# Moments of later columns taken ahead of most of the first fold, roots in three batches of four, folds and first transforms moved

## The chip, the cores and the metric

The kernel runs on one core of a Trainium2 chip. The metric is device microseconds (us) of one execution. A time is the median of several runs; most runs of one kernel agree within 0.3%. "Span" is the profiled execution from its first to its last instruction; it is about 1.7 to 1.8 us shorter than the timed value.

Names: PE is TensorE, DVE is VectorE, ACT is ScalarE, POOL is GpSimd, SP is SyncE.

## The reference

```python
x  = A_x                                  # 1 x 2048 x 512, bf16
xn = layernorm(x)                         # over the 512 features
a  = irfft2(rfft2(xn) * (w_r + 1j*w_i))   # over rows and features
b  = (gelu(xn @ w_gate) * (xn @ w_up)) @ w_down    # inner width 1792
return x + a + b
```

## The kernel before

The 2048 rows are 16 "columns" of 128 rows. Four columns make a block. PE computes the gated unit (`glu`: gate and up products, 14 slices of the inner width for each block) for block 0, then blocks 1 to 3, and then the down projection. The spectral part (fold, products `bp` with the row transform, feature transforms, filter, inverse) is interleaved with the units of `glu`. Before a block's units can start, its four columns are normalized: moments on DVE, `1/sqrt` by Newton steps on POOL ("roots"), normalization on ACT, transposes by DMA.

```python
def rsqrt(V, y, var, n):                  # V is POOL for columns 4 to 15
    v = pc.tile([P, n], F32, name=f"v{n}"); t = ...
    V.tensor_scalar(out=v[:], in0=var, scalar1=EPS, ...)
    V.tensor_scalar(out=yi, in0=vi, scalar1=-0.5, scalar2=float(0x5F3759DF), ...)
    for _ in range(3):                    # Newton steps, 4 operations each on POOL
        ...
def moments(c):                           # DVE: "stats", then "mv"
    tc.keep_in_program_order(V.bn_stats(out=stats[:], in_=x_t[:, c, :]))
    V.bn_aggr(out=mv[:, c, :], in_=stats[:])
# ... (cut)
def normalize(c):                         # columns 4 to 15: ACT, waits for rstd and nb of POOL
    tc.keep_in_program_order(
        nc.scalar.activation(out=xn[:, c, :], in_=x_t[:, c, :], func=AF.Identity,
                             bias=nb[:, c:c + 1], scale=rstd[:, c:c + 1]))
def fold(cg):                             # DVE, four steps: A, A, xf, xf; needs xn of 4 columns
    ...
def pstep(cg, q):                         # PE: products bp of fold cg; ACT copies them to Bs
    ...
def glu(c0, n, fc):                       # PE: 4 + 4 matmuls
    gp = ps.tile(..., name="g_ps", tag="G", bufs=2)
    up = ps.tile(..., name="u_ps", tag="U", bufs=2)
    # ... matmuls (cut)
    nc.scalar.activation(out=ge[:], in_=gp[:], func=AF.Gelu_apprx_tanh)              # ACT frees g_ps
    nc.vector.tensor_tensor(out=hT[sb, fc][:, o:o + w], in0=up[:], in1=ge[:], ...)   # DVE frees u_ps

# the schedule: (time in units, task); a unit of four columns and one slice counts 1.724
for c0, n, t in ((4, 4, 8), (8, 8, 14)):
    for c in range(c0, c0 + n):
        j = c - c0
        tasks.append((t + 0.8 * j, lambda c=c: moments(c)))
        tasks.append((t + n + 5 + 0.9 * j, lambda c=c: (normalize(c), transposes(c, 1))))
    tasks.append((t + n - 0.5, lambda c0=c0, n=n: scales(nc.gpsimd, c0, n)))
for cg in range(4):
    t = (8, 21, 30.5, 34)[cg]
    tasks.append((t, lambda cg=cg: fold(cg)))
    for q in range(4):
        tasks.append((t + (3 + q if cg < 2 else 1.5 + 0.6 * q), lambda cg=cg, q=q: pstep(cg, q)))
t0, dt = 38, 5.5                          # first feature transforms
```

Each engine works through its instructions in one fixed order, made when the program is built; an instruction that waits holds up everything behind it on that engine. And `g_ps` and `u_ps` have two buffers each: PE can be one unit ahead of ACT's gelu and of DVE's `hT`, not more.

Of the kernel before, what the change touches and what calls it, by code (L numbers as in the profile page):

```python
# [10 lines left out]
P = 128  # L11
BF16 = mybir.dt.bfloat16
F32 = mybir.dt.float32
# [110 lines left out]
def kernel(  # L124
# [11 lines left out]
    nc = tc.nc  # L136
# [11 lines left out]
    pc = ctx.enter_context(tc.tile_pool(name="pc", bufs=1))  # L148
    ps = ctx.enter_context(tc.tile_pool(name="ps", bufs=2, space=bass.MemoryType.PSUM))
    pw = ctx.enter_context(tc.tile_pool(name="pw", bufs=2))  # L150
# [79 lines left out]

    def rsqrt(V, y, var, n):

        v = pc.tile([P, n], F32, name=f"v{n}")
        t = pc.tile([P, n], F32, name=f"t{n}")
        V.tensor_scalar(out=v[:], in0=var, scalar1=EPS, scalar2=None, op0=ALU.add)
        vi, yi = v[:].bitcast(I32), y.bitcast(I32)
        V.tensor_scalar(out=yi, in0=vi, scalar1=-0.5, scalar2=float(0x5F3759DF), op0=ALU.mult, op1=ALU.add)
        for _ in range(3):
            V.tensor_tensor(out=t[:], in0=y, in1=y, op=ALU.mult)
            if V is nc.vector:  # L240
                V.scalar_tensor_tensor(out=t[:], in0=v[:], scalar=-0.5, in1=t[:],
                                       op0=ALU.mult, op1=ALU.mult)
                V.scalar_tensor_tensor(out=y, in0=t[:], scalar=1.5, in1=y,
                                       op0=ALU.add, op1=ALU.mult)
                continue
            V.tensor_tensor(out=t[:], in0=v[:], in1=t[:], op=ALU.mult)
            V.tensor_scalar(out=t[:], in0=t[:], scalar1=-0.5, scalar2=1.5, op0=ALU.mult, op1=ALU.add)
            V.tensor_tensor(out=y, in0=t[:], in1=y, op=ALU.mult)
# [5 lines left out]
    def moments(c):  # L254
        V = nc.vector
        stats = pw.tile([P, V.BN_STATS_DIM], F32, name="stats")
        tc.keep_in_program_order(V.bn_stats(out=stats[:], in_=x_t[:, c, :]))  # L257
        V.bn_aggr(out=mv[:, c, :], in_=stats[:])

    def scales(V, c0, n):  # L260
        r, b = rstd[:, c0:c0 + n], nb[:, c0:c0 + n]
        rsqrt(V, r, mv[:, c0:c0 + n, 1], n)
        if c0 >= 4:
            V.tensor_tensor(out=b, in0=mv[:, c0:c0 + n, 0], in1=r, op=ALU.mult)
            V.tensor_scalar(out=b, in0=b, scalar1=-1.0, scalar2=None, op0=ALU.mult)  # L265

    def normalize(c):
        if c < 4:
            nc.vector.tensor_scalar(out=xn[:, c, :], in0=x_t[:, c, :], scalar1=mv[:, c, 0:1],
                                    scalar2=rstd[:, c:c + 1], op0=ALU.subtract, op1=ALU.mult)  # L270
        else:
# [3 lines that stand above are left out]
# [26 lines left out]
    def transposes(c0, n):  # L301
        if c0 < 4:
            tp = ps.tile([P, NE, n, P], BF16, name="tp", tag="S", bufs=4)
            for j in range(n):
                for e in range(NE):
                    nc.tensor.transpose(tp[:, e, j, :], xn[:, c0 + j, e * P:(e + 1) * P], ident)  # L306
            return nc.vector.tensor_copy(out=xnT[0][:, :, c0:c0 + n, :], in_=tp[:])
        else:
            for j in range(c0, c0 + n):
                nc.sync.dma_start_transpose(out=xnT[j // 4][:, :, j % 4, :], in_=xn[:, j, :])  # L310
# [4 lines left out]
    def fold(cg):  # L315
        V = nc.vector
        xs = xn[:, 4 * cg:4 * cg + 4, :]
        lo, hi = xs[:, :, 0:256], xs[:, :, 511:255:-1]
        A = pw.tile([P, 4, 2, 256], BF16, name="A", bufs=1)
        V.tensor_tensor(out=A[:, :, 0, :], in0=lo, in1=hi, op=ALU.add)  # L320
        V.tensor_tensor(out=A[:, :, 1, :], in0=lo, in1=hi, op=ALU.subtract)
        xf = pw.tile([P, 4, 4, P], BF16, name="xf")
        V.tensor_tensor(out=xf[:, :, 0:4:3, :], in0=A[:, :, :, 0:128], in1=A[:, :, :, 255:127:-1],  # L323
                        op=ALU.add)
        V.tensor_tensor(out=xf[:, :, 2:0:-1, :], in0=A[:, :, :, 0:128], in1=A[:, :, :, 255:127:-1],
                        op=ALU.subtract)
        fold_out[cg] = xf

    def pstep(cg, q):
        xf = fold_out[cg]  # L330
        bp = ps.tile([P, 4, P], F32, name="bp", tag="S", bufs=4)
        for j in range(4):
            nc.tensor.matmul(bp[:, j], lhsT=xf[:, j, q, :], rhs=RF_t[:, 4 * cg + j, :],  # L333
                             start=True, stop=True)
        o = Bs[:, q].rearrange("p g c r a -> p (c r) g a")[:, 8 * cg:8 * cg + 8]
        evac(o, bp[:].rearrange("p c (r g a) -> p (c r) g a", r=2, a=4))
# [174 lines left out]


    tasks = [(20, load_tables), (28, gather_tables)]
    for c0, n, t in ((4, 4, 8), (8, 8, 14)):
        for c in range(c0, c0 + n):
            j = c - c0
            tasks.append((t + 0.8 * j, lambda c=c: moments(c)))
            tasks.append((t + n + 5 + 0.9 * j, lambda c=c: (normalize(c), transposes(c, 1))))
        tasks.append((t + n - 0.5, lambda c0=c0, n=n: scales(nc.gpsimd, c0, n)))
    for cg in range(4):  # L520
        t = (8, 21, 30.5, 34)[cg]
        tasks.append((t, lambda cg=cg: fold(cg)))
        for q in range(4):
            tasks.append((t + (3 + q if cg < 2 else 1.5 + 0.6 * q), lambda cg=cg, q=q: pstep(cg, q)))
    tasks.append((36, tables_fix))
    t0, dt = 38, 5.5
    for i, g in enumerate((1, 2, 3, 4, 5, 6, 7, 0)):
        tasks.append((t0 + dt * i, lambda g=g: dstep(2 * g)))
        tasks.append((t0 + dt * i + 1, lambda g=g: dstep(2 * g + 1)))
# [50 lines left out]
```

## Time and profile before

185.42 us median (185.33 to 185.53, 4 runs).

| read from | what | value |
|---|---|---|
| page, part 1 | PE busy | 172.2 of 183.8 us (94%) |
| page, part 1 | DVE / ACT / POOL busy | 116.1 / 97.8 / 17.2 us |
| timeline of PE | first matmul | 5.68 us |
| timeline of PE | third set of transposes to first inverse product | 15.03 to 124.25: 109.2 us |

The last row is the stretch in which the change acts. Its two ends in the timeline of PE:

```profile
15.03 0.72 PE L306 MATMUL tp<-CT,xn 128*128 128x128 bf16 x8
...
124.25 0.83 PE L445 MATMUL yp<-CT,Gs 128*128 128x128 bf16 x12
```

Both kernels do the same matmuls in it, so its length is a good measure of what PE lost there. "Lost" below is time between the starts of two matmuls beyond the usual step (0.216 us for 512 columns, 0.055 for 128).

The view of windows of the kernel before, two stretches; the columns are the stretch, its length, then busy time and number of instructions of PE, PE's weight loads, DVE, ACT and POOL, then granted clock, DMA share and GB/s:

```profile
14.50:36.20 21.70, 21.57 (x160) 14.31 (x158) 19.25 (x50) 12.75 (x26) 3.28 (x17) 1.00 0.68 203
36.20:60.14 23.94, 22.78 (x143) 11.22 (x144) 14.27 (x23) 18.90 (x34) 13.69 (x32) 1.00 0.66 121
```

PE is full up to 36 us and loses over 1 us after it. The timeline of PE (start us, length us, engine, line, operation, output<-inputs, sizes, count; in brackets the idle time and what ended it) names the two large losses: at 36.0 us block 1 waits for transposed columns, and at 48.2 us the products of the third fold wait for `xf` of DVE.

```profile
35.15 1.03 PE L480 MATMUL u_ps<-xnT,Wu_sb 128*128 128x512 bf16 x4
36.72 1.02 PE L477 MATMUL g_ps<-xnT,Wg_sb 128*128 128x512 bf16 x4 [0.55 <-DMA xnT<-xn]
...
47.98 0.38 PE L477 MATMUL g_ps<-xnT,Wg_sb 128*128 128x512 bf16 x1
48.96 0.40 PE L333 MATMUL bp<-RF_t,xf 128*128 128x128 bf16 x4 [0.60 <-DVE xf L323]
```

The timeline of POOL shows the first and last operation of each of the two root batches, and two operations in the middle of the second:

```profile
24.46 0.24 POOL L235 TENSOR_SCALAR v<-mv 128x4 f32<-128x4 f32 x1 [24.03 <-DVE mv L258]
...
28.70 0.23 POOL L265 TENSOR_SCALAR nb<-nb 128x4 f32<-128x4 f32 x1
36.16 0.60 POOL L235 TENSOR_SCALAR v<-mv 128x8 f32<-128x8 f32 x1 [7.22 <-DVE mv L258]
...
37.40 0.20 POOL L239 TENSOR_TENSOR t<-rstd 128x8 f32<-128x8 f32 x1
...
37.97 0.55 POOL L247 TENSOR_SCALAR t<-t 128x8 f32<-128x8 f32 x1
...
41.73 0.24 POOL L265 TENSOR_SCALAR nb<-nb 128x8 f32<-128x8 f32 x1
```

The first batch takes 24.46 to 28.93 us, the second 36.16 to 41.97 us. The operations of one batch have the same work, but some take 0.20 us and others 0.48 to 0.60.

### The profile page before, as it was taken

Reading aid. Unit: us, or ns where it says so; the run is one execution under the profiler, and the core shown is the slowest. Engines: PE = TensorE matmul, PEld = TensorE weight load, DVE = VectorE, ACT = ScalarE, POOL = GpSimd, SP = SyncE. Lnnn points to the kernel's source line nnn. Section 1 sums busy time; section 2 is a strip of 40 time slices with the busy share of each in tenths; the row PEclk is TensorE's granted clock in tenths of the full one; section 3 lists DMA queues with packets and bytes.
Section 4 is the critical chain, followed back from the end, with each engine's and each line's share of the span. In section 5 each row is a group of like instructions: output and inputs, shape, how many; then the busy total and the mean of one; then the engine's idle time right before and its main releaser. Section 6 shows DMA issues by size and latency. Waiting matters only on the chain.

```text
span 183.8 us, 3059 instructions
## 1 busy us (share of the span) xinstructions
PE 172.2 (94%) x1080; PEld 92.7 (50%) x1080; DVE 116.1 (63%) x273; ACT 97.8 (53%) x181; POOL 17.2 (9%) x52
## 2 busy tenths in 40 slices
PE   0699999899899999999999999999999999999991
PEld 0598974354445544554555554445445445445440
DVE  2679959972954599679778879835541541541611
ACT  2533568559888986988988875453211211211100
POOL 0000042177642000000000000000000000000000
PEclk9999999999999999999999999999999999999998
DMA  4999971404995001201392210100122221221210
GB/s 147 325 384 382 339 181 30 86 0 110 227 136 159 0 13 44 62 14 43 80 356 83 59 48 13 44 13 2 61 83 67 78 86 62 76 95 60 83 57 29
DMA packets 22062, 19.37 MB, mean 105 GB/s; under 512 B 8288, under 2 KB 20576, under 8 KB 22048
## 3 DMA queue, kind: packets, MB, share of 16 engines
q1 hardware_dynamic: 20816, 17.22, 33.2%
q0 software_dynamic: 416, 1.32, 3.1%
q10 hardware_dynamic: 816, 0.66, 1.1%
q8 instruction: 8, 0.13, 0.3%
q14 instruction: 6, 0.05, 0.1%
HBM read 13.41 MB, written 2.10 MB: 84 GB/s over the span
## 4 chain that ended last, share of the span: by engine, by line
PE 83%; DVE 4%; DMA 3%; POOL 3%; issue 3%; ACT 2%; ACTq 0%
PE y_ps L490 26%; PE g_ps L477 22%; PE u_ps L480 22%; DMA Wu_sb<-in_B_w_up_dram 3%; PE dp L346 2%; PE ep L358 2%; PE yp L445 2%; PE gp L430 2%; PE y_ps L492 2%; DVE hT L484 2%; PE bp L333 2%; ACT xn L273 1%; ACT ge L483 1%; DVE stats L257 1%; PE tp L306 1%
## 5 line engine op out<-in xcount | busy, mean ns | idle before, releaser
L477 PE MATMUL g_ps<-xnT,Wg_sb 128*128 128x512 bf16 (+2 forms) x276 | 62.3, 347 | 1.1 <-DMA xnT<-xn 0.5
L480 PE MATMUL u_ps<-xnT,Wu_sb 128*128 128x512 bf16 (+2 forms) x276 | 60.9, 344 | 0.1
L490 PE MATMUL y_ps<-Wd_sb,hT 128*128 128x512 bf16 x224 | 51.0, 379 | 0.0
L484 DVE TENSOR_TENSOR hT<-u_ps,ge 128x512 bf16<-128x512 f32 (+2 forms) x69 | 40.1, 583 | 15.0 <-PE u_ps L480 7.5
L483 ACT ACTIVATE ge<-g_ps 128x512 bf16<-128x512 f32 (+2 forms) x69 | 35.5, 520 | 21.2 <-PE g_ps L477 19.6
L480 PEld LDWEIGHTS <-Wu_sb 128*128 128x128 bf16 x276 | 26.6, 101 | 23.1 <-DMA Wu_sb<-in_B_w_up_dram 0.4
L477 PEld LDWEIGHTS <-Wg_sb 128*128 128x128 bf16 x276 | 25.8, 102 | 19.6 <-issue 2.0
L490 PEld LDWEIGHTS <-hT 128*128 128x128 bf16 x224 | 21.3, 98 | 23.1
L495 DVE TENSOR_TENSOR y_sb<-y_ps,y_sb 128x512 bf16<-128x512 f32 x16 | 11.1, 692 | 30.2 <-PE y_ps L492 30.2
L451 ACT CAST yf<-yp 128x512 bf16<-128x512 f32 x16 | 9.2, 587 | 37.3 <-PE yp L445 37.3
L361 ACT CAST E<-ep 64x512 bf16<-64x512 f32 x32 | 18.5, 579 | 3.7 <-PE ep L358 3.4
L339 ACT CAST Bs<-bp 128x512 bf16<-128x512 f32 x16 | 9.0, 586 | 3.4 <-PE bp L333 3.4
L339 ACT CAST ds<-dp 128x512 bf16<-128x512 f32 x16 | 9.2, 607 | 1.2 <-PE dp L346 1.2
L273 ACT ACTIVATE xn<-x_t,nb,rstd 128x512 bf16<-128x512 bf16 x12 | 9.4, 810 | 0.4 <-POOL nb L265 0.4
L339 ACT CAST Gs<-gp 128x512 bf16<-128x512 f32 x16 | 8.6, 591 | 1.4 <-PE gp L430 1.4
L257 DVE BATCH_NORM_STATS2 stats<-x_t 128x6 f32<-128x512 bf16 x14 | 9.2, 667 | 0.0
L383 DVE TENSOR_TENSOR X<-E 128x512 bf16<-128x512 bf16 x8 | 3.4, 426 | 8.6 <-ACT E L361 8.6
L306 PE MATMUL tp<-CT,xn 128*128 128x128 bf16 x16 | 2.0, 266 | 5.8 <-DVE xn L291 5.7
L445 PEld LDWEIGHTS <-Gs 128*128 128x128 bf16 x64 | 4.8, 98 | 3.3
L492 PE MATMUL y_ps<-yt,RI_t 128*128 128x512 bf16 x16 | 6.1, 379 | 0.0
L346 PE MATMUL dp<-CT,Bs 128*128 128x128 bf16 x64 | 6.0, 219 | 0.0
L333 PE MATMUL bp<-RF_t,xf 128*128 128x128 bf16 x64 | 5.4, 219 | 0.6 <-DVE xf L323 0.6
(67 smaller groups left out, 120.3 us busy)
## 6 DMA issues: line engine op xcount, KB each, us to landing
y_sb<-in_A_x_dram SPq DMA_DIRECT2D x16, 128.0 KB, 2.1
F<-F SPq DMA_DIRECT2D x32, 64.0 KB, 2.0
out_dram<-y_sb SPq DMA_DIRECT2D x16, 128.0 KB, 1.7
Wd_sb<-in_B_w_down_dram SPq DMA_DIRECT2D x1, 1792.0 KB, 8.8
x_t<-in_A_x_dram SPq DMA_DIRECT2D x3, 512.0 KB, 11.7
Wg_sb<-in_B_w_gate_dram SPq DMA_DIRECT2D x1, 768.0 KB, 9.0
Wu_sb<-in_B_w_up_dram SPq DMA_DIRECT2D x1, 768.0 KB, 10.6
Wg_sb<-in_B_w_gate_dram SPq DMA_DIRECT2D x2, 256.0 KB, 5.1
```

The source lines that it names most:

```text
L257: tc.keep_in_program_order(V.bn_stats(out=stats[:], in_=x_t[:, c, :]))
L273: nc.scalar.activation(out=xn[:, c, :], in_=x_t[:, c, :], func=AF.Identity, bias=nb[:, c:c + 1], scale=rstd[:, c:c + 1]))
L339: nc.scalar.copy(out=o, in_=i)
L346: nc.tensor.matmul(dp[:, q // 2, q % 2, :], lhsT=Bs[:, q, G].rearrange("p c r a -> p (c r a)"), rhs=FQ[q], start=(q == 0), stop=(q == 3), ...
L361: nc.scalar.copy(out=E[64 * h:64 * h + 64, r], in_=ep[64 * r:64 * r + 64])
L477: nc.tensor.matmul(gp[:], lhsT=Wg_sb[:, e, fc * P:(fc + 1) * P], rhs=rhs[:, e, :], start=(e == 0), stop=(e == NE - 1))
L480: nc.tensor.matmul(up[:], lhsT=Wu_sb[:, e, fc * P:(fc + 1) * P], rhs=rhs[:, e, :], start=(e == 0), stop=(e == NE - 1))
L483: nc.scalar.activation(out=ge[:], in_=gp[:], func=AF.Gelu_apprx_tanh)
L484: nc.vector.tensor_tensor(out=hT[sb, fc][:, o:o + w], in0=up[:], in1=ge[:], op=ALU.mult)
L490: nc.tensor.matmul(y_ps[:], lhsT=hT[sb, f][:, cl * P:(cl + 1) * P], rhs=Wd_sb[:, f, :], start=(f == 0), stop=False)
L492: nc.tensor.matmul(y_ps[:], lhsT=late["RI"][:, c, :], rhs=late["yt"][:, c, :], start=False, stop=True)
L495: nc.vector.tensor_tensor(out=y_sb[:], in0=y_ps[:], in1=y_sb[:], op=ALU.add)
```

## The change

Intent: take the moments of columns 4 to 7 earlier, so that block 1 doesn't wait; split the second root batch so that columns 8 to 11 don't wait for 12 to 15; place folds and transforms accordingly.

```diff
-        v = pc.tile([P, n], F32, name=f"v{n}")
-        t = pc.tile([P, n], F32, name=f"t{n}")
+        v = pw.tile([P, n], F32, name=f"v{n}")
+        t = pw.tile([P, n], F32, name=f"t{n}")
@@ the schedule
-    for c0, n, t in ((4, 4, 8), (8, 8, 14)):
-        for c in range(c0, c0 + n):
+    for c0, tm, ts, tx in ((4, 6, 9.5, 14.3), (8, 15, 18.5, 23.5), (12, 19, 23, 28)):
+        for c in range(c0, c0 + 4):
             j = c - c0
-            tasks.append((t + 0.8 * j, lambda c=c: moments(c)))
-            tasks.append((t + n + 5 + 0.9 * j, lambda c=c: (normalize(c), transposes(c, 1))))
-        tasks.append((t + n - 0.5, lambda c0=c0, n=n: scales(nc.gpsimd, c0, n)))
+            tasks.append((tm + 0.8 * j, lambda c=c: moments(c)))
+            tasks.append((tx + 0.9 * j, lambda c=c: (normalize(c), transposes(c, 1))))
+        tasks.append((ts, lambda c0=c0: scales(nc.gpsimd, c0, 4)))
     for cg in range(4):
-        t = (8, 21, 30.5, 34)[cg]
+        t = (12, 22, 29.5, 34)[cg]
@@
-    t0, dt = 38, 5.5
+    t0, dt = 39.5, 5.5
```

The tiles `v4` and `t4` are now used by three batches; `pw` holds two buffers of each name, `pc` only one. The first two folds come later in the schedule, the third one unit sooner, the transforms 1.5 units later.

## The prediction

> **What bounds it.** TensorE. The table of five stretches shows it busy 8.2 of the first 14.5 us, 21.57 of 21.70 (to 36.2), 22.78 of 23.94 (to 60.1), then gapless to 124.4. The change can only win back PE time lost between 15 and 60 us. By start-to-start times in PE's timeline (a 512-column matmul takes 0.216 us, a set of four 0.86, a fold product `bp` of four 0.22) the losses are: 0.71 us at 36.0 (block 1 waits for the transposed `xnT`, landing 36.59), 0.77 + 0.2 at 48.2 (third fold's `bp` waits for `xf`), and about 0.8 in small slips from 53 to 59.6, where products and single matmuls alternate. Sum about 2.5 us, 1.3% of 185.4.
>
> **What it moves.** Nothing is removed; POOL gets 16 more small operations (three root batches of 4 instead of 4 and 8). The static order shows: moments of columns 4 to 7 go ahead of three of the first fold's four DVE steps, and need not wait for data (landed at 12.75 us). The first fold's products move behind a 512-column unit; the third fold's `bp` stand after the 4th unit of block 1 on PE instead of the 7th; the alternation is gone.
>
> **Walk with traced durations** (moment pair 0.68 to 0.81 us, fold step 0.60, `hT` 0.34 or 0.59, normalize 0.71, gelu 0.49, copy 0.48, roots 4.5 a batch; an estimate). Moments 4 to 7 are done at 21.6 instead of 24.4, roots at 26.2 to 27.2, transposes land by about 35, before PE asks at 36.1: the 0.71 us gap goes. Roots may take up to 1 us longer because fold steps on DVE now run beside them: in the old second batch POOL operations took 0.48 to 0.60 us beside fold steps and 0.20 otherwise, which agrees with the Trainium skill, "SBUF — State Buffer", section "SBUF: two separate sides", on the exclusive port pair of VectorE and GpSimd. But moments, first and second folds now share 28 to 39 us with `hT` on one in-order DVE, so the `hT` at the block boundary comes near 39 us: PE waits 0.4 to 1 us. The second root batch ends at 38.8 to 40.3 (before, all eight at 41.97), the third at 43 to 45, later than before. ACT does xn 8 to 11 with gelus and copies between, so the third fold's `xf` comes at 46 to 47.7 (before 48.9), while PE reaches its `bp` already at 44 to 45.8: a wait of 1 to 2 us, larger than 0.77. Net over 15 to 60 us: 0.1 us gained to 1.4 lost. The constants look tuned, which argues for a gain; I weigh the two.
>
> **Prediction: 185.8 us**, 8 in 10 between 184.2 and 187.2. Faster by over 2%: 0.02; within 2%: 0.94; slower by over 2%: 0.04.
>
> **What would show it.** Right: no PE wait for `xnT` at 36 us; moments of columns 4 to 7 from 17.5 us; POOL batches from near 21.6, 34 to 35 and 39 to 40; a PE wait for `hT` near 38 to 40; a PE wait of over 1 us for the third fold's `xf` between 44 and 48; PE gapless from 60 us. Wrong: PE busy from 36 to 60 would mean about 183 us.
>
> **What would make it wrong.** If the second roots end before 38.5, the main wait falls below 1 us. If the transforms, shifted 1.5 schedule units later, delay the inverse at 124.4, it costs about 0.5 us.

## More of the kernel before

ACT hardly waits for the second batch here; its timeline:

```profile
42.00 0.81 ACT L273 ACTIVATE xn<-x_t,nb,rstd 128x512 bf16<-128x512 bf16 x1 [0.37 <-POOL nb L265]
```

## The result

186.79 us median (186.73 to 187.27, 4 runs) against 185.42. The ratio is 1.0066, with a 95% interval of 1.0043 to 1.009: within 2%, and a little slower beyond noise. (A ratio is the mean time of one kernel's runs over the mean of the other's of the same rounds, so it is not quite the ratio of the medians.) Executions over 1.5% slower than the fastest of the same kernel are left out of the means.

The same two stretches of the changed kernel, in the view of windows:

```profile
14.50:36.20 21.70, 21.10 (x157) 14.27 (x157) 18.29 (x44) 12.21 (x26) 5.18 (x19) 1.00 0.70 206
36.20:60.14 23.94, 21.05 (x132) 10.78 (x133) 14.86 (x28) 17.87 (x32) 15.14 (x46) 1.00 0.53 122
```

DVE and ACT do no more work than before; PE loses more. (The trace of this run lacks 18 of PE's 1080 matmuls, one about every 9 us, so a PE busy sum is slightly low; the length of the stretch doesn't suffer from that.) The stretch from the third transposes to the first inverse product is longer by 1.62 us, 110.83 against 109.21, which is the result; what lies outside it differs by 0.4 us the other way. (In the profiled runs, the part from the first inverse product to the end takes 59.5 to 59.6 us in three, the kernel before, e1 and e10, and 59.1 to 59.2 in the other eleven. So this 0.4 us doesn't go with the change; why it comes and goes was not looked into. Where a time and a stretch differ by 0.4 us below, it is this.) Its two ends in the timeline of PE, the changed kernel:

```profile
15.00 0.72 PE L306 MATMUL tp<-CT,xn 128*128 128x128 bf16 x8
...
125.83 0.83 PE L445 MATMUL yp<-CT,Gs 128*128 128x128 bf16 x12
```

The timeline of PE at the places that answer to those of before:

```profile
33.85 1.02 PE L480 MATMUL u_ps<-xnT,Wu_sb 128*128 128x512 bf16 x4 [0.43 <-DVE hT L484]
...
36.44 1.03 PE L477 MATMUL g_ps<-xnT,Wg_sb 128*128 128x512 bf16 x4
...
40.14 1.02 PE L480 MATMUL u_ps<-xnT,Wu_sb 128*128 128x512 bf16 x4 [0.47 <-DVE hT L484]
...
44.11 1.02 PE L477 MATMUL g_ps<-xnT,Wg_sb 128*128 128x512 bf16 x3 [0.26 <-ACT ge L483]
44.97 1.03 PE L480 MATMUL u_ps<-xnT,Wu_sb 128*128 128x512 bf16 x4
47.83 0.40 PE L333 MATMUL bp<-RF_t,xf 128*128 128x128 bf16 x4 [1.83 <-DVE xf L323]
```

The wait of block 1 for the transposed columns is gone: its first set starts at 36.44, right behind the set before it. But PE now waits for `hT` (33.85 and 40.14), for a gelu (44.11), and 1.83 us for `xf` of the third fold (47.83), where the kernel before waited 0.60.

The timeline of POOL, first and last operation of each of the three batches, and one operation beside a fold step:

```profile
21.63 0.58 POOL L235 TENSOR_SCALAR v<-mv 128x4 f32<-128x4 f32 x1 [21.19 <-DVE mv L258]
...
26.93 0.23 POOL L265 TENSOR_SCALAR nb<-nb 128x4 f32<-128x4 f32 x1
35.16 0.23 POOL L235 TENSOR_SCALAR v<-mv 128x4 f32<-128x4 f32 x1 [7.99 <-DVE mv L258]
...
35.75 0.55 POOL L239 TENSOR_TENSOR t<-rstd 128x4 f32<-128x4 f32 x1
...
40.12 0.23 POOL L265 TENSOR_SCALAR nb<-nb 128x4 f32<-128x4 f32 x1
40.43 0.23 POOL L235 TENSOR_SCALAR v<-mv 128x4 f32<-128x4 f32 x1
...
44.68 0.23 POOL L265 TENSOR_SCALAR nb<-nb 128x4 f32<-128x4 f32 x1
```

The first batch starts 2.8 us earlier than before, at 21.63. The second ends at 40.35, only 1.6 us earlier than the old one, although it has half the columns; the third ends at 44.91, 2.9 us later than all of them ended before. The timeline of ACT shows what the second batch does to it:

```profile
35.77 0.60 ACT L483 ACTIVATE ge<-g_ps 128x512 bf16<-128x512 f32 x1 [1.51 <-PE g_ps L477]
40.39 0.81 ACT L273 ACTIVATE xn<-x_t,nb,rstd 128x512 bf16<-128x512 bf16 x1 [4.02 <-POOL nb L265]
41.11 0.57 ACT L483 ACTIVATE ge<-g_ps 128x512 bf16<-128x512 f32 x1
...
47.97 0.62 ACT L483 ACTIVATE ge<-g_ps 128x512 bf16<-128x512 f32 x1
```

ACT stands 4.02 us before xn of column 8, from 36.37 to 40.39. Behind it in the queue is the gelu of block 1's first unit (41.11), whose product was complete at 37.5 us (its set starts at 36.44 in the timeline of PE). From 40.4 to about 53 us ACT then has no gap: it works off what piled up.

The waits for `hT` begin earlier, and in a similar way. ACT waits 0.73 us for the first roots, the gelu behind this runs from 29.10 us, and DVE waits 1.41 us for that gelu; the timelines of ACT and of DVE:

```profile
27.20 0.81 ACT L273 ACTIVATE xn<-x_t,nb,rstd 128x512 bf16<-128x512 bf16 x1 [0.73 <-POOL nb L265]
```

```profile
29.71 0.69 DVE L484 TENSOR_TENSOR hT<-u_ps,ge 128x512 bf16<-128x512 f32 x1 [1.41 <-ACT ge L483]
```

From 29.71 to 40.09 us DVE has no gap. PE loses 0.38 (one missing record taken off), 0.25 and 0.64 us, 1.27 in all, at 33.85, 37.55 and 40.14, each time before a set for `u_ps`, which waits until an `hT` frees a buffer. The gelus that these `hT` need had run by 36.4 us, so these 1.27 us don't come from the 4.02 us wait of ACT.

### The profile page after: what moved, and what is told of

It is laid out like the page before. It is cut to its first block, busy times and chain, and to the rows that moved or that the text cites. A ratio compares the mean times of both kernels' runs of the same rounds, so it can differ in the third digit from the quotient of the medians.

```text
span 185.0 us, 3057 instructions
## 1 busy us (share of the span) xinstructions
PE 170.8 (92%) x1062; PEld 93.0 (50%) x1080; DVE 116.3 (63%) x273; ACT 97.7 (53%) x181; POOL 20.5 (11%) x68
## 4 chain that ended last, share of the span: by engine, by line
PE 85%; DVE 4%; issue 3%; POOL 2%; ACT 2%; DMA 2%; ACTq 0%
PE y_ps L490 26%; PE g_ps L477 23%; PE u_ps L480 23%; PE yp L445 2%; PE dp L346 2%; PE gp L430 2%; PE ep L358 2%; PE y_ps L492 2%; DMA x_t<-in_A_x_dram 2%; PE bp L333 2%; PE tp L306 1%; DVE hT L484 1%; ACT ge L483 1%; DVE stats L284 1%; ACT Bs L339 1%
## 5 line engine op out<-in xcount | busy, mean ns | idle before, releaser
L477 PE MATMUL g_ps<-xnT,Wg_sb 128*128 128x512 bf16 (+2 forms) x264 | 60.1, 345 | 1.4 <-DVE xnT L307 0.5
L333 PEld LDWEIGHTS <-xf 128*128 128x128 bf16 x64 | 4.4, 98 | 4.7 <-DVE xf L323 2.3
L445 PE MATMUL yp<-CT,Gs 128*128 128x128 bf16 x64 | 5.9, 219 | 0.1
```

What stands on the lines that cost most here:

```text
L333: nc.tensor.matmul(bp[:, j], lhsT=xf[:, j, q, :], rhs=RF_t[:, 4 * cg + j, :], start=True, stop=True)
L445: nc.tensor.matmul(yp[:, q], lhsT=Gs[:, q, c], rhs=IQ[q], start=(q == 0), stop=(q == 3), skip_group_check=True)
L477: nc.tensor.matmul(gp[:], lhsT=Wg_sb[:, e, fc * P:(fc + 1) * P], rhs=rhs[:, e, :], start=(e == 0), stop=(e == NE - 1))
```

## The experiments

Theory after the result: PE's losses between 33 and 50 us come from the chain moments, roots, normalize, fold, and from instructions standing in order behind a wait in it. Rivals: the fold and transform times; the place of the third fold's products on PE; a plain lack of DVE or ACT throughput; waiting roots because of the port pair that the prediction names.

Before each run the built instruction orders were compared, because moving one task can let the scheduler reorder others. Where "the order is the same" is said, that was checked on the built program.

All runs, with the PE stretch of the profiled run (third transposes to first inverse product). The ratio is to the kernel before on the same chip.

| run | time us | ratio (95%) | chip | PE stretch us |
|---|---|---|---|---|
| kernel before | 185.42 | | first | 109.21 |
| changed kernel | 186.79 | 1.0066 (1.0043 to 1.009) | first | 110.83 |
| a0_again | 186.65 | 1.0057 (1.0036 to 1.0078) | A | 110.80 |
| e1_two_steps | 184.78 | 0.9962 (0.994 to 0.9984) | A | 108.51 |
| e2_third_fold_later | 186.58 | 1.0056 (1.0032 to 1.008) | A | 110.49 |
| e3_before_two_steps | 184.65 | 0.996 (0.9935 to 0.9986) | A | 108.76 |
| e4_fold_times_back | 188.00 | 1.001 (0.9971 to 1.0049) | B | 112.13 |
| e5_normalize_later | 185.97 | 0.9904 (0.9864 to 0.9945) | B | 110.23 |
| e6_moments_into_gap | 185.02 | 0.9852 (0.9813 to 0.9892) | B | 109.08 |
| e7_moments_all_early | 186.11 | 0.9908 (0.987 to 0.9946) | B | 110.28 |
| a1_again | 186.74 | 1.0057 (1.0044 to 1.0071) | C | 110.80 |
| e8_gap_again | 185.21 | 0.9983 (0.9967 to 0.9999) | C | 108.95 |
| e9_third_sooner | 183.26 | 0.9877 (0.9862 to 0.9892) | C | 107.22 |
| e10_third_sooner_two_steps | 183.08 | 0.9872 (0.9855 to 0.9889) | C | 106.86 |

On chip A the kernel before ran at 185.38 us, on C at 185.67, but on B at 187.66 (187.09 to 189.07). Why is open: its four slowest runs there had a granted clock of 0.986 to 0.989, but the other seven, at 0.995 to 1.0, still took 187.09 to 187.84. The other kernels did not show it, as far as one repeat can tell: e6 on B and its repeat e8 on C have 185.02 and 185.21. So the ratios of chip B are not used; its four runs are compared with each other and by their PE stretch.

### a0_again and a1_again: the changed kernel once more

No edit. Expected:

> The changed kernel itself, for reference on the same chip. It should repeat: about 1.2 to 1.4 us over the kernel before, PE waiting 1.83 us for the third fold's xf near 46 to 48 us, ACT waiting 4.0 us for the second root batch. If the loss of 0.7% is noise of one chip, it will be under 0.3% here.

> The changed kernel once more, so that the two versions below are compared with it and with the kernel before on one chip (on the last chip the kernel before ran at 187.7 us, 2 us above the other chips, while the others did not look slow). Expected 186.6 to 186.9 if the chip is like the first two, with the 4.0 us wait of ACT for the second roots.

Measured: 1.0057 both times, and the same PE stretch of 110.80 us. The loss is real and not one of a chip. (a1_again's profiled run, the slowest of its six with 188.0 us, started its third transposes 1.1 us later than the others; the stretch after that is unchanged.)

### e1_two_steps: shorten only the roots

```diff
-        for _ in range(3):
+        for _ in range(3 if V is nc.vector else 2):
```

> The changed kernel with two Newton steps instead of three on POOL: each root batch has 4 operations less, about 1.1 us (0.28 us each). The order on PE, DVE and ACT is the same as in the changed kernel. Theory (the loss is the wait of PE's static third-fold products for a chain moments, roots, normalize, fold): the wait of 1.83 us falls to about 0.5, most of the 0.43 and 0.47 us waits for hT go too, and the time falls 1.3 to 1.8 us, to about 185.2. Rival (the loss is VectorE being full between 28 and 39 us, or the later transforms): the time stays within 0.4 us of the changed kernel, since DVE's work is the same.

The result stays correct. Measured: 184.78 against 186.65, so 1.87 us faster, with the order on PE, DVE and ACT the same; a little more than expected. The second roots end at 37.82 instead of 40.35 us, and ACT's wait for them shrinks from 4.02 to 2.07 us; its 0.73 us wait for the first roots is gone, and of the 1.27 us that PE lost to `hT`, 0.43 are left. The stretch is 2.29 us shorter. The timelines of ACT and of PE in this run:

```profile
37.85 0.81 ACT L273 ACTIVATE xn<-x_t,nb,rstd 128x512 bf16<-128x512 bf16 x1 [2.07 <-POOL nb L265]
```

```profile
45.29 0.40 PE L333 MATMUL bp<-RF_t,xf 128*128 128x128 bf16 x4 [1.05 <-DVE xf L323]
```

The wait for `xf` is still 1.05 us, not the 0.5 expected. What follows: root latency is on the critical path (it sets when PE can go on). DVE's work and the instruction order did not change, so a lack of DVE throughput alone can't be the cause.

### e2_third_fold_later: move only the place where the wait shows

```diff
-        t = (12, 22, 29.5, 34)[cg]
+        t = (12, 22, 31.5, 34)[cg]
```

> The changed kernel with the third fold scheduled 2 units later (31.5 instead of 29.5): on PE its products stand after the 6th unit of block 1 instead of the 4th; DVE and ACT orders barely differ. Theory (PE's static place of these products makes the wait): the 1.83 us wait for xf disappears; ACT's backlog of gelus gives part of it back as waits for ge near 48 us, so about 1.0 us is won, about 185.8. Rival (the stage is limited by ACT or DVE throughput, the place does not matter): no gain, within 0.3 us of the changed kernel.

Measured: 186.58 against 186.65, no gain. My theory lost this point. The wait for `xf` did vanish, as expected, but the timeline of PE shows most of it back in other places (the first line is a wait that the changed kernel has too, at 44.11):

```profile
44.24 1.02 PE L477 MATMUL g_ps<-xnT,Wg_sb 128*128 128x512 bf16 x3 [0.26 <-ACT ge L483]
...
46.40 1.02 PE L477 MATMUL g_ps<-xnT,Wg_sb 128*128 128x512 bf16 x4 [0.28 <-ACT ge L483]
...
48.78 1.02 PE L477 MATMUL g_ps<-xnT,Wg_sb 128*128 128x512 bf16 x4 [0.40 <-ACT ge L483]
...
50.50 0.83 PE L333 MATMUL bp<-RF_t,xf 128*128 128x128 bf16 x12
...
53.91 0.40 PE L333 MATMUL bp<-RF_t,xf 128*128 128x128 bf16 x4 [0.20 <-ACT Bs L339]
```

New are the waits for gelus at 46.40 and 48.78 (0.28 and 0.40) and for a copy of ACT at 53.91 (0.20), with smaller slips between those. ACT is without a gap from 40.5 to 53.0 us in this run too, behind the same 4.02 us wait. So the third fold's products are only where the delay of ACT's queue shows; the cause is upstream. That made the theory sharper: ACT stands in order behind a root result, and the work behind it piles up.

### e3_before_two_steps: are roots critical in the kernel before too?

Same edit as e1, on the kernel before.

> The kernel before with two Newton steps instead of three on POOL, instruction order on the other engines the same. Theory (the chain through the roots also made the waits of the kernel before, 0.71 us for the transposes and 0.77 for xf): both shrink by up to their whole size, the time falls 0.8 to 1.5 us to about 184.2. Rival (only the new arrangement is sensitive to the roots): no change over 0.3 us.

Measured: 184.65 against 185.38, 0.73 us faster, just under the expected range. The stretch is 0.45 us shorter; the rest of the difference lies outside it. The wait for `xf` shrank (0.77 and 0.2 us lost before, 0.34 and 0.15 now), but the wait for the transposed columns did not. The first roots end at 27.64 us there and xn of column 4 starts at 28.75: on ACT it stands behind a gelu that waits for PE. Here an earlier result was of no use to an instruction that wasn't next in its queue.

Set beside e1 this says more: with the shorter roots in both, the changed kernel takes 184.78 us and the kernel before 184.65 on the same chip, with stretches of 108.51 and 108.76. So nearly all of the 1.27 us that the change cost on this chip (186.65 against 185.38) hangs on how long the roots take.

### e4_fold_times_back: undo the moved folds and transforms

```diff
-        t = (12, 22, 29.5, 34)[cg]
+        t = (8, 21, 30.5, 34)[cg]
@@
-    t0, dt = 39.5, 5.5
+    t0, dt = 38, 5.5
```

> The changed kernel with the fold and transform times of the kernel before: only the new moments, roots and normalize times are left. New theory (ACT's in-order queue puts the gelu of block 1's first unit behind xn of column 8, which waits 4.0 us for the second roots; the backlog after it is the loss): that order stays, so the loss stays, 186.2 to 186.9 us. Rival (the moved folds and transforms cost the time): back to about 185.4.

Measured: 188.00, on the chip where the others were not slow; its stretch is 112.13 us, 1.3 longer than the changed kernel's. So the moved folds and transforms were not what cost the time; with the new moments they saved some. How much is less certain: the run was not repeated on another chip, and on this one the kernel before, which has the same fold times, ran slow for a reason that is open. The expected 186.2 to 186.9 was too low. ACT waits 4.40 us for the second roots in this run, and PE's waits for a gelu are longer (0.70 and 1.41 us):

```profile
42.05 1.02 PE L477 MATMUL g_ps<-xnT,Wg_sb 128*128 128x512 bf16 x4 [0.70 <-ACT ge L483]
...
47.07 1.02 PE L477 MATMUL g_ps<-xnT,Wg_sb 128*128 128x512 bf16 x3 [1.41 <-ACT ge L483]
```

The opposite half, the kernel before with the new fold times, could not be run whole: with the third fold at 29.5 it would read column 11 before that is normalized (at 27 + 3 × 0.9 = 29.7), and the simulator refuses the program for reading a part of `xn` that was not yet written.

### e5_normalize_later: take the gelu out from behind the wait

```diff
-    ... (8, 15, 18.5, 23.5), ...
+    ... (8, 15, 18.5, 25.5), ...
```

> The changed kernel with the normalizations of columns 8 to 11 issued 2 units later (25.5 instead of 23.5): ACT now does one gelu and one copy of block 1 in the idle time before xn of column 8; DVE's order is nearly the same; on PE the third fold's products stand as in the run e2_third_fold_later. New theory: the gelu no longer waits for the roots, about 1 us less backlog, so 0.7 to 1.2 us better than e2_third_fold_later, about 185.6. Rival (the root results are simply too late, whatever stands before them in ACT's queue): within 0.3 us of that run's 186.6.

Measured: 185.97, against e2's 186.58 on another chip; by the stretch, 110.23 against 110.49, the gain is only 0.26 us. ACT's longest wait for roots fell to 0.96 us, as expected. But PE then waits 1.16 us for a gelu at 47.93; this gelu starts on ACT at 47.30, behind two normalizations in a row, and two more follow it. This fits the theory of the queue, with normalizations now piled up a few us later, but it is not a proof; the verdict is unclear. Removing a wait from ACT's queue without having the roots earlier gains little.

### e6_moments_into_gap and its repeat e8_gap_again: have the second roots early

DVE had idle time of 1.3 and 1.4 us between 25 and 29.7 us in the changed kernel. The edit puts the moments of columns 8 to 11 there:

```diff
-    ... (8, 15, 18.5, 23.5), ...
+    ... (8, 11.5, 14.5, 19.5), ...
```

> The changed kernel with the moments of columns 8 to 11 moved 3.5 units earlier, into the 2.7 us in which DVE idles between 25 and 29.7 us, and their roots and normalizations 4 units earlier; columns 12 to 15, folds and transforms as in the changed kernel, and PE's order identical to it. Theory (roots of columns 8 to 11 are late because their moments stand behind hT on DVE): roots end near 34 instead of 40.3, no ACT wait of 4 us, no PE wait for xf or ge over 0.3 us; 183.2 to 184.0, better than both kernels. Rival (DVE or ACT has too much work between 28 and 52 us in any order): no better than 186.

> e6_moments_into_gap again: 184.7 to 185.2 us; against the changed kernel on the same chip 1.5 to 2 us faster, against the kernel before about 0.3% faster or the same. Its ACT waits 3.0 us for the third roots, PE 1.1 and 0.4 us for gelus near 48 and 50 us.

Measured: 185.02 and 185.21. Against the changed kernel on the same chip C, e8 is 1.5 us faster. PE's order is the same as in the changed kernel, so this gain is of DVE's and ACT's orders and of the earlier roots. The second roots end at 33.64 (e6), ACT doesn't wait for them, and the waits for `xf` are gone. The expected 183.2 to 184.0 was missed, because the third roots were now in the way; the timeline of ACT in e6:

```profile
41.61 0.60 ACT L483 ACTIVATE ge<-g_ps 128x512 bf16<-128x512 f32 x1
45.18 0.81 ACT L273 ACTIVATE xn<-x_t,nb,rstd 128x512 bf16<-128x512 bf16 x1 [2.97 <-POOL nb L265]
...
47.08 0.58 ACT L483 ACTIVATE ge<-g_ps 128x512 bf16<-128x512 f32 x1
```

Again a gelu (47.08) stands behind a normalization that waits for roots, 2.97 us here, and PE waits for it:

```profile
47.72 1.02 PE L477 MATMUL g_ps<-xnT,Wg_sb 128*128 128x512 bf16 x4 [0.93 <-ACT ge L483]
```

### e7_moments_all_early: everything earlier

```diff
-    ... (8, 15, 18.5, 23.5), (12, 19, 23, 28)
+    ... (8, 11.5, 14.5, 19.5), (12, 15, 18.5, 24)
```

> As e6_moments_into_gap, and the moments, roots and normalizations of columns 12 to 15 earlier as well (15, 18.5, 24); PE's order again the same. Theory: now xn of column 12 stands before the gelu of block 1's first unit on ACT and waits for the third roots near 40 us, so part of the wait comes back for another column: PE waits about 1 us near 41; 184.2 to 184.9, between e6 and the kernel before. Rival (earlier moments are always better): at or under e6.

Measured: 186.11, 1.1 us slower than e6 on the same chip. The third roots end at 41.45, 3.7 us earlier than in e6, and still the kernel is slower: xn of column 12 now stands before the gelu of block 1's first unit on ACT. The timelines of ACT and PE:

```profile
36.92 0.58 ACT L483 ACTIVATE ge<-g_ps 128x512 bf16<-128x512 f32 x1
41.48 0.81 ACT L273 ACTIVATE xn<-x_t,nb,rstd 128x512 bf16<-128x512 bf16 x1 [3.97 <-POOL nb L265]
42.20 0.57 ACT L483 ACTIVATE ge<-g_ps 128x512 bf16<-128x512 f32 x1
```

```profile
42.82 0.38 PE L477 MATMUL g_ps<-xnT,Wg_sb 128*128 128x512 bf16 x1 [2.09 <-ACT ge L483]
```

ACT waits 3.97 us, PE 2.09. The direction was as expected, the size was not (1 us of wait expected). "Earlier is better" is refuted: what counts here is which instruction stands behind which wait.

### e9_third_sooner: third roots earlier, ACT's order untouched

```diff
-    ... (8, 11.5, 14.5, 19.5), (12, 19, 23, 28)      # e8
+    ... (8, 11.5, 14.5, 19.5), (12, 17, 20.5, 28)
```

> e8 with the moments and roots of columns 12 to 15 two units earlier (17 and 20.5), their normalizations left at 28: the orders on PE and ACT are identical to e8's, on DVE the last moment stands before the second fold's second half. Theory (what is lost is ACT standing in order before a root result): the third roots end near 42.5 instead of 45.2, ACT waits under 0.5 us, PE's waits from 40 to 52 us go to under 0.4 us: 1.0 to 1.4 us faster than e8, about 183.7, and faster than both kernels. Rival (ACT is simply overloaded from 40 to 52 us): at most 0.3 us faster than e8.

Measured: 183.26 (4 runs), 1.95 us faster than e8, 3.5 us faster than the changed kernel and 2.4 us faster than the kernel before (0.9877 of it). That is more than the 1.0 to 1.4 us expected. The orders on PE and ACT are those of e8; only DVE's differs, and the roots. Which part of the gain comes from DVE's new order itself was not separated. The view of windows:

```profile
36.20:60.14 23.94, 23.94 (x152) 12.43 (x151) 14.55 (x24) 18.66 (x34) 13.63 (x32) 1.00 0.51 117
```

PE has no idle time from 36.2 to 60.14 us. ACT still waits 1.47 us for the third roots, more than the 0.5 expected, since these start at 36.87 beside fold steps and end at 43.46, not 42.5; but the gelus reach PE in time:

```profile
43.49 0.81 ACT L273 ACTIVATE xn<-x_t,nb,rstd 128x512 bf16<-128x512 bf16 x1 [1.47 <-POOL nb L265]
```

The rival, ACT overloaded from 40 to 52 us in any order, allowed 0.3 us and is refuted.

### e10_third_sooner_two_steps: are the roots still critical?

Same edit as e1, on e9.

> e9 with two Newton steps on POOL, orders on PE, DVE and ACT identical to e9's. In the changed kernel this was worth 1.87 us. Theory: in e9 nothing important waits for roots any more, so it is worth under 0.4 us here. Rival (two steps help by freeing POOL or the port pair wherever roots stand): again about 1 us or more.

Measured: 183.08 against 183.26, a gain of 0.18 us, where the same edit was worth 1.87 us in the changed kernel and 0.73 in the kernel before. The runs of the two overlap (182.93 to 183.76 against 183.23 to 183.35), so 0.18 us is not clear of noise; the stretch is 0.36 us shorter. In e9 ACT still waits for the third roots, but the wait no longer reaches PE, and so shorter roots are worth next to nothing. The stretch of 106.86 us is about what PE needs when it loses nothing; against it the kernel before lost 2.35 us, the changed kernel 3.97 (109.21 and 110.83 less 106.86).

## Why the prediction was right

The measured 186.79 lies in the predicted range (184.2 to 187.2), and within 2% was given 0.94. Point by point:

- **"The 0.71 us gap goes."** Right: block 1's first set starts at 36.44 without a wait for DMA.
- **First moments from 17.5 us, roots from near 21.6 to 26.2 to 27.2.** Right: 17.48, 21.63 and 27.16.
- **Roots slowed beside fold steps.** Right: in the first batch three operations took 0.54 to 0.58 us, in the second two took 0.55 and 0.56, the others 0.19 to 0.23. The first batch took 5.53 us, against 4.47 before. No run took the port pair away by itself, so its share in the loss (0.7 us of the second batch at most, two times 0.35) is read from the trace and not tested.
- **Second roots end at 38.8 to 40.3, third at 43 to 45.** Right at the edge: 40.35 and 44.91. They start at 35.16 and 40.43, 0.2 and 0.4 us after the latest times given (34 to 35, 39 to 40).
- **PE waits 0.4 to 1 us for `hT` near 38 to 40.** Right: 0.64 us lost at 40.14, and 0.25 and 0.38 earlier, at 37.55 and 33.85, of which the prediction did not speak.
- **A wait of 1 to 2 us for the third fold's `xf`, PE arriving at 44 to 45.8.** Right: 2.0 us lost, from 45.83 to 47.83 (1.83 shown as idle).
- **Gapless from 60 us, the inverse not delayed.** Right.
- **The size.** The walk said 0.1 us gained to 1.4 lost, and 1.37 was lost. The middle of the walk is 0.65 us lost, or 186.07; the guess ("the constants look tuned"), which was no measurement, took a further 0.3 us off. So of the 1.0 us by which 185.8 was too low, 0.3 are the guess and 0.7 the walk.
- **Luck in the size.** By start-to-start times the changed kernel loses 0.38, 0.25 and 0.64 us to `hT`, 0.29 and 0.43 to gelus (41.73 and 44.11) and 2.0 to `xf`, 3.99 in all. The walk named only the 0.64 and the 2.0, so 1.35 us of loss were not foreseen. Against them stand the small slips of about 0.8 us, which are gone, and which the walk's sum seems to leave out: 1.4 to 3.0 us of new waits less the two large old losses (0.71 and 0.97) make 0.3 us gained to 1.3 lost, close to what it states. Two omissions of opposite sign kept the result inside the walk.
- **"If the second roots end before 38.5, the main wait falls below 1 us."** Nearly: in e1 they ended at 37.82 and PE lost 1.2 us there; in e6, at 33.64, and this wait was gone.
- **"PE busy from 36 to 60 would mean about 183 us."** e9 later met this condition, with 183.26 us.

The chain that makes the third fold late (roots, normalizations, fold) was in the prediction, and e1 confirms it. What the prediction did not see is what else stands behind that chain. It took the order of ACT's queue as given, gelus and copies between the normalizations, and named no wait of PE for a gelu. The runs show ACT idle for 4 us with a gelu that was due held behind a normalization: moving the fold's products gains nothing (e2), while another order of DVE with earlier roots turns the loss into a gain (e9).

## What to carry to other kernels

When a tuned pipeline loses time in a wait on the busiest engine, look at the engine that it waits for, and ask what stood before the late instruction in that engine's fixed order: here gelus stood behind a normalization that waited for roots, and removing the visible wait on PE (e2) only moved it. Place an instruction that waits for a long chain behind the work that is already due, and start its chain in idle time of the engine that feeds it; starting everything earlier (e7) can put the wait in front of urgent work. Then test by shortening the chain: if that gains next to nothing (e10), this chain is no longer what limits.

## What the Trainium skill lacked or had wrong

- "SBUF — State Buffer", section "Who interferes with whom", says that a DVE instruction with two SBUF inputs contends with a GpSimd instruction that reads SBUF and one with at most one SBUF input outside the 2-port modes does not. The traces agree: POOL operations of 0.20 us took 0.48 to 0.60 us beside fold steps (two SBUF inputs), and stayed at 0.19 to 0.20 beside moments, which read one (37.51 to 38.76 us in the changed kernel). The page lacks a figure for small arithmetic operations of GpSimd: in the changed kernel the held ones ended 0.05 to 0.09 us after the DVE instruction beside them.
- "Perfetto Trace Analysis", section "Optimization Strategy", advises finding the gaps of the most contended engine and what released them. It lacks the case of e2: the gap of 1.83 us ended by `xf` was removed and the time stayed (186.58 against 186.65 us), because the releasing engine was itself behind after a 4.02 us wait with due work in its queue.
- No page that I read says that matmul records can be missing at a steady pace: 9 of the 14 traces here have 1062 of 1080, which shows as single steps of twice 0.216 us about every 9 us.
- "TensorE: Matmul & The Clock Gate", section "Wait — 56ns, not 53.3ns?", gives 215.7 ns between starts of warm 512-column matmuls; the traces agree, with 0.86 us for a set of four. The same page's section "Back-to-back issue gap" names a sustained 131 ns for such pairs of weight load and matmul; every run here shows 0.216.
